# Pooled attention and a snake layer on one core: other places for loads, a store, filler products and a normalisation

## The chip, the cores and the metric

The kernel runs on one core of one Trainium2 chip. The time is the device time of one execution in microseconds (us). Of the kernel before there are ten executions; their median is 920.99 us, the lowest 916.61 and the highest 925.30.

The engines of the core are TensorE (PE in the profile; PEld is its loading of weights), VectorE (DVE), ScalarE (ACT), GpSimd (POOL) and SyncE (SP), whose only work here is to issue DMAs. Each has its own stream of instructions and works through it in order. They wait for each other by semaphores.

## What is computed

Two layers follow each other, in float32 throughout. In the first, k and v are averaged over groups of 8 positions, so that 576 positions become 72, and all 576 queries of each of 8 batches and 8 heads attend to them. In the second, the 4608 rows of 512 numbers go through a layer of 2048 hidden units.

```python
batch, n_heads, seq, head_dim = (8, 8, 576, 64)
k_p = k.reshape(B, H, Sp, pool, D).mean(axis=3)          # pool = 8, Sp = 72
v_p = v.reshape(B, H, Sp, pool, D).mean(axis=3)
scores = scale * np.matmul(q, k_p.transpose(0, 1, 3, 2))
scores = scores - np.max(scores, axis=-1, keepdims=True)
attn = np.exp(scores)
attn = attn / (np.sum(attn, axis=-1, keepdims=True) + 1e-09)
x = np.matmul(attn, v_p).transpose(0, 2, 1, 3).reshape(B * S, H * D)
h = x @ w_in                                             # 4608 x 512 by 512 x 2048
s = np.sin(alpha * h)
out = (h + s * s / (alpha + 1e-09)) @ w_out              # 2048 x 512
```

## The kernel before

**The second layer sets the frame.** The rows of x are taken in nine tiles u of 512 rows. Both of its matrix products use a scheme with 7 products of half-size blocks in place of 8. `hidden` (from L742) walks through 28 slots for each u: four groups J of hidden units, seven products k in each, in the order 1, 5, 6, 2, 7, 3, 4. A slot's product is 4 matmuls of 128x256, each of two passes (L767). Its operands are blocks of w_in or sums of them (`combine_w_in`, L638, which writes the tiles s1, s2, a21 and s4 of a group), and blocks of x or differences of them (`sums_of_x`, L740).

What ScalarE and VectorE do with a product's result is put off by one slot: `left0` to `left6` are the seven pieces (copies of partial sums, adds L746, sine, square), and piece k is written out at the start of slot k+1. `left1` finishes the group before (`finish`, L834), and `left2` stores it into a buffer in DRAM (`store_g`, L841), from which a last phase (`outputs`, L1087) reads it.

**The first layer is spread over these slots.** `carry(u)` says what is put ahead of which slot's product; for each u it prepares the attention of batch b = u+1. In their order: the score products (`two_scores`, L289, two bursts of 32 and 48 short matmuls), row maxima and differences (L312, L313), exponentials (L338), sums and the product with their reciprocals (`norm`, L344 to L346, the last on GpSimd), transposes of the weights in blocks of 32 (`turn`, L472 to L482), 16 DMAs that put the turned blocks in place (`move`, L492), and the products with v (`all_values`, L565 and L578), which write the next tile of x. `k_t` (L251) transposes the pooled k of the batch after next for its scores.

k and v are loaded in halves of a batch (L108; L131 and L139) and pooled by three adds on GpSimd (`pool_rows`, L120). k's and v's first parts share a pool of two buffers, "kvin". The queries are loaded (L80, L96), turned by VectorE and 16 more DMAs (`turn_q`, L212, L219). All these DMAs are issued by SP in the order in which they are written, and SP waits in place when one of them must wait. It is not tied to the slots otherwise: a DMA whose data are there is issued as soon as those ahead of it are.

**The first batch has its own code.** `first_batch` loads k, q and v of batch 0 by pairs of heads, and TensorE pools and transposes them (`k_head` L355, `k_last` L361, `q_head` L372, `sum_v_rest` L182, `sum_v_rows` L192). For each of four pairs follow the products (`products_head`, L393), `soft_shift` (maximum L399 and difference L401), `soft_exp` (L407) and `norm_head` (sum L413, reciprocal L414, two multiplications L419). `a_head` transposes the weights (L447, copied by L449; the last eight keys L455, L456), and `values` (L535, L537) multiplies them with v; `to_x` (L506) copies the result to x. The first half of x is made in `first_batch`, the second in slot 2 of u = 0. Six products of the identity with itself (`warm`, L868), whose results are not used, stand ahead of it in two groups of three, around the transpose of alpha (L600).

The whole order is written by hand; no scheduler changes it.

Of the kernel before, what the change touches and what calls it, by code (L numbers as in the profile page):

```python
# [13 lines left out]
F32 = mybir.dt.float32  # L14
# [26 lines left out]
class Kernel:  # L41
# [79 lines left out]

    def load_v(self, b, i):

        nc, D, H = self.nc, self.D, self.H
        if b not in self.vp:
            self.vp[b] = self.ap.tile([P, H // 2, D], F32, name="vm", bufs=2), self.ap.tile([P, H // 2, D], F32, name="vz", bufs=2)
        vm, vz = self.vp[b]
        if i == 0:
            t = self.kvp.tile([P, 2048], F32, name="kvin")[:].rearrange("p (h x) -> p h x", h=4)
            for s in range(2):  # L130
                nc.sync.dma_start(out=t[64 * s:64 * s + 64],  # L131
                                  in_=self.v[b, 4 * s:4 * s + 4, 0:4 * P, :].rearrange("h (p t) d -> p h (t d)", t=POOL))
            self.pool_rows(t, vm[:])
            return
        x = self.kvp.tile([P, POOL * D], F32, name="vr", bufs=1)[:]
        for s in range(2):
            for c in range(2):
                r = 64 * s + 32 * c
                nc.sync.dma_start(out=x[r:r + 32], in_=self.v[b, 4 * s:4 * s + 4, 4 * P:, :].rearrange("h (k t) d -> h k (t d)", t=POOL))  # L139
        self.pool_rows(x, x[:, 0:D])  # L140
        nc.gpsimd.tensor_tensor(out=vz[:], in0=x[:, 0:D].unsqueeze(1).to_broadcast([P, H // 2, D]),
                                in1=self.mask[:].unsqueeze(2).to_broadcast([P, H // 2, D]), op=OP.mult)

# [87 lines left out]
    def attention(self, b):  # L231
# [208 lines left out]

        def a_head(g, banks, between=None):

            aM, aR = a0_views()
            for e in range(2):
                ps = self.psum([P, 4, P], banks[e])
                for t in range(4):
                    nc.tensor.transpose(ps[:, t, :], self.a0[:, t, 2 * g + e].rearrange("p s k -> p (s k)"), self.ident[:])  # L447
                cp = nc.vector.tensor_copy if g and e else nc.scalar.copy
                cp(out=aM[:, 2 * g + e, 0:4 * P], in_=ps.rearrange("k t n -> k (t n)"))  # L449
            if between:  # L450
                between()
            ps = self.psum([P, 4, P], banks[2])
            w = 64 * g + 64
            for t in range(4):
                nc.tensor.transpose(ps[:w, t, :], self.z0[:, t].rearrange("p hp x k -> p (hp x k)")[:, 0:w], self.ident[:])  # L455
            nc.scalar.copy(out=aR[w - 64:w, 0:4 * P], in_=ps[w - 64:w].rearrange("k t n -> k (t n)"))  # L456
# [36 lines left out]

        def to_x(ps, hp, t0, m, s0=0):

            while s0 < m:
                u, x0 = divmod(b * S + t0 + s0, 2 * TH)
                w = min(m - s0, 2 * TH - x0)
                if u not in self.xT:
                    self.xT[u] = self.home(u % 3, [P, self.K1, 2 * TH])  # L500
                x = self.xT[u][:, hp, x0:x0 + w]
                if t0:
                    y = ps[..., s0:s0 + w]
                else:
                    x, y = x.rearrange("p (j t) -> p j t", t=4), ps[:, s0 // 4:(s0 + w) // 4, :]
                nc.scalar.mul(out=x, in_=y, mul=1.0 / POOL)  # L506
                s0 += w
# [20 lines left out]

        def values(hps, banks, n=1):

            ps = [self.psum([P, 4 * P], i) for i in banks]
            parts = [value_parts(hp, False) for hp in hps]
            for o, (main, _) in zip(ps, parts):
                for e, (w, x) in enumerate(main):
                    nc.tensor.matmul(o[64 * e:64 * e + 64], w, x, start=True, stop=False, skip_group_check=True)  # L535
            for o, (_, (w, x)) in zip(ps, parts):
                nc.tensor.matmul(o, w.rearrange("p e d -> p (e d)"), x, start=False, stop=True, skip_group_check=True)  # L537
            for i in range(n):
                for hp, o in zip(hps, ps):
                    to_x(o.rearrange("p (t j) -> p j t", t=4), hp, 0, 512 // n * (i + 1), 512 // n * i)  # L540

# [189 lines left out]

    def sums_of_x(self, u, n):

        nc = self.nc
        if u not in self.bt:
            self.bt[u] = self.home(3, [P, 4, 2, TH])
        xT, bt = self.xT[u], self.bt[u]
        B = lambda i, j: xT[:, 2 * i:2 * i + 2, j * TH:(j + 1) * TH]
        o, x, y = ((0, B(0, 1), B(0, 0)), (1, B(1, 1), bt[:, 0]), (2, B(1, 1), B(0, 1)), (3, B(1, 0), bt[:, 1]))[n]
        nc.vector.tensor_tensor(out=bt[:, o], in0=x, in1=y, op=OP.subtract)  # L740

    def hidden(self, u, extra):  # L742
# [5 lines left out]
        for slot in range(7 * self.NJ):  # L748
# [51 lines left out]

            def left2(G=G, Q=before):
                if Q:
                    self.store_g(Q)
                G.b7 = bank()
                nc.scalar.copy(out=G.b7[:], in_=G.b6[:])
                G.p5 = self.tp.tile([P, JW, TH], F32, name="p5")
                nc.scalar.copy(out=G.p5[:], in_=G.b5[:])
# [7 lines left out]

            def left5(G=G):
                add(G.g[:, 0, :, 1], G.b6[:], G.p5[:])
# [34 lines left out]
    def first_batch(self):  # L852
# [12 lines left out]
        add_k = [self.load_k_heads(0, nc.sync, nc.vector)]  # L865
        one = self.sm.tile([P, 1], F32, name="one")
        nc.scalar.activation(out=one[:], in_=self.ident[:, 0:1], func=AF.Sqrt)
        warm = lambda n, i: [nc.tensor.matmul(self.psum([P, P], i), self.ident[:], self.ident[:], start=True, stop=True) for _ in range(n)]  # L868
        warm(3, 3)
        self.turn_alpha()  # L870
# [12 lines left out]
        for hp in range(1, 4):  # L883
            add_k.append(self.load_k_heads(hp, nc.sync, nc.vector if hp < 2 else nc.gpsimd))
            self.load_q_heads(0, 2 * hp, 2 * hp + 2)
        add_rest()
        self.load_v_rows(0, h[0][:], self.tp.tile([P, self.DM], F32, name="p5")[:])
# [3 lines left out]
        A.new_a()  # L891
        warm(3, 3)
        A.k_head(0)
        A.q_head(0)
        A.k_last()
        for f in add_k[1:]:
            f()
        A.products_head(0)
        A.k_head(1)
        A.q_head(1)  # L900
        A.soft_shift(0)
        refine()
        A.q_head(2)
        A.products_head(1)
        A.soft_exp(0)
        A.soft_shift(1)
        A.norm_head(0, nc.gpsimd)
        A.k_head(2)
        A.q_head(3)
        A.soft_exp(1)  # L910
        A.products_head(2)
        A.norm_head(1, nc.vector)
        A.k_head(3)
        A.soft_shift(2)
        A.products_head(3)
        A.soft_exp(2)
        self.sum_v_rest(0, 0)
        A.soft_shift(3)
        A.norm_head(2, nc.gpsimd)
        self.sum_v_rows(0, 0, 2)  # L920
        A.a_head(0, (1, 7, 0), lambda: A.soft_exp(3))
        self.sum_v_rows(0, 1, 2)
        A.norm_head(3, nc.gpsimd)
        self.load_q_rest(0, self.q_rest)
# [3 lines left out]
        self.load_w_in_part(1)  # L928
        A.values((0, 1), (4, 1), 2)
        self.combine_w_in(0, (0, 1))  # L930
        self.combine_w_in(0, (2, 3), nc.gpsimd)
        self.sums_of_x(0, 0)

    def carry(self, u):
# [5 lines left out]
        if u == 0:  # L940
            A0, A = self.att[:2]
            at(2, A0.rest_q)
            at(2, A0.a_head, 1, (5, 6, 7))
            at(2, self.half_k)
            at(2, A0.values, (2, 3), (2, 1))
            at(2, self.sums_of_x, 0, 1)
            at(2, A0.score, 4)
# [8 lines left out]
            at(4, A.k_t)  # L956
            at(7, self.load_v, 1, 0)
            at(7, self.load_v, 1, 1)
            for i in range(2):
# [5 lines left out]
            for i in range(4):  # L965
                at((9, 9, 15, 15)[i], A.exp, i)
                at((10, 10, 16, 16)[i], A.norm, i)
                at((13, 13, 17, 19)[i], A.turn, i)
            at(8, self.combine_w_in, 2, (0, 1, 2, 3), self.nc.gpsimd)
            at(10, self.combine_w_in, 3, (0, 1, 2, 3), self.nc.gpsimd)  # L970
            at(17, A0.norm_rest)
            at(23, A0.a_rest)
            at(24, lambda: A0.values_rest((5, 6, 7, (self.turn + 1) % 5)))
            for r in (32, 96):
                at(3, self.nc.gpsimd.memset, self.aM[r:r + 32, :, 704:736], 0.0)
            at(19, A.move, 0)
            at(19, A.move, 1)
            at(26, A.all_values)
# [9 lines left out]
        if 0 < u < last:  # L988
# [8 lines left out]
            at(14, A.move, 0)  # L997
            at(14, A.move, 1)
            for i in range(2):
                at((0, 1)[i], self.load_v, b, i)  # L1000
                if b < last:
                    at(12, self.load_k, b + 1, i)
            at(25, A.all_values)
# [327 lines left out]
```

## Time and profile before

| | us |
|---|---|
| median of ten executions | 920.99 |
| the profiled execution, its own time | 919.92 |
| its span, from the first to the last instruction | 918.1 |
| first product of `hidden` (L767) starts | 21.95 |
| value products of batch 1 (L565) start | 84.55 |
| value products of batch 2 start | 140.54 |
| last product of `hidden`, first phase, ends (start of the last phase, L1087 alone) | 537.1 |

The profile is of one execution. A line of a timeline or of the chain of waits begins with the start and the duration in us, counted from the start of the span; then come engine, line, operation, what is written and read, the number of instructions that were put together, and in brackets how long the engine had been idle and what ended that. "SPq" is SP issuing DMAs. A line of windows gives a stretch, its length, the busy time of PE, PEld, DVE, ACT and POOL with the number of instructions, then the granted share of the TensorE clock, the busy share of the 16 DMA engines and what they moved in GB/s. A matmul's end is modelled, so starts say more than durations there.

The DMA engines are busiest at the start: 0.98 of the first 45 us, in which 255 GB/s are moved; between 104 and 400 us their share is 0.57 to 0.69.

### The profile page before, as it was taken

The page shows a single profiled execution, that of the slowest core. Times are in us where ns is not written, and L with a number is a line of the kernel's source. Part 1 is how long each engine was busy: PE and PEld are TensorE (multiplying, and loading weights), DVE is VectorE, ACT ScalarE, POOL GpSimd, SP SyncE. Part 2 cuts the span into 40 slices and gives each one's busy share as a digit, 9 for nine tenths or more (in the row PEclk, how much of TensorE's full clock was granted, in tenths as well). Part 3 has the DMA queues.
Part 4 walks back from the last instruction along what each step waited for, and adds up shares of the span by engine and source line. Part 5 has one row for each costly group of instructions (what it writes and reads, how often), then busy time and mean ns, then how long its engine had stood idle before and what let it go on. Part 6 is the DMA issues. An engine that isn't in the chain of part 4 may idle for free.

```text
span 918.1 us, 17704 instructions
## 1 busy us (share of the span) xinstructions
PE 901.4 (98%) x7001; PEld 818.3 (89%) x7001; DVE 667.5 (73%) x1005; ACT 435.4 (47%) x997; POOL 162.7 (18%) x155
## 2 busy tenths in 40 slices
PE   8999999999999999999999999999999999999997
PEld 6786887887878888888888899999999999999997
DVE  7674766746667566673466889978888888979894
ACT  5595685866758667586886631112111112111111
POOL 4694250612507034040000000000000000000000
PEclk9999999999999999999999999999999999999999
DMA  9957666766666656637327237171617263533401
GB/s 254 246 190 190 186 175 179 217 177 187 196 171 203 177 155 167 187 93 263 136 92 247 92 107 223 37 224 26 223 37 191 68 170 89 161 98 120 139 14 39
DMA packets 134730, 141.12 MB, mean 154 GB/s; under 512 B 49832, under 2 KB 103224, under 8 KB 134648
## 3 DMA queue, kind: packets, MB, share of 16 engines
q1 hardware_dynamic: 133304, 138.54, 51.9%
q10 hardware_dynamic: 1344, 1.45, 0.6%
q8 instruction: 55, 0.90, 0.4%
q14 instruction: 27, 0.22, 0.1%
HBM read 75.37 MB, written 47.19 MB: 133 GB/s over the span
## 4 chain that ended last, share of the span: by engine, by line
PE 89%; DMA 4%; SPq 3%; POOL 2%; issue 1%; DVE 0%; ACT 0%; POOLq 0%; ACTq 0%
PE PS L767 43%; PE PS L1087 41%; PE PS L565 2%; PE PS L289 2%; DMA a<-in_moe_w_in_dram 2%; DMA kvin<-in_k_dram 1%; DMA kvin<-in_v_dram 1%; SPq L632 1%; POOL as L638 1%; PE PS L578 1%; SPq L492 0%; POOL kvin L120 0%; POOL ex L346 0%; SPq L96 0%; DMA aM<-tr 0%
## 5 line engine op out<-in xcount | busy, mean ns | idle before, releaser
L767 PE MATMUL PS<-home,a 128*128 128x256 f32 x1152 | 264.4, 381 | 0.9 <-ACT home L506 0.5
L767 PEld LDWEIGHTS PS<-home,a 128*128 128x128 f32 x1152 | 216.5, 190 | 37.4 <-issue 5.0
L767 PE MATMUL PS<-home,as 128*128 128x256 f32 x864 | 200.3, 381 | 2.9 <-issue 1.6
L767 PEld LDWEIGHTS PS<-home,as 128*128 128x128 f32 x864 | 162.7, 190 | 26.5 <-issue 2.6
L1087 PE MATMUL PS<-s,wb 128*128 128x144 f32 x896 | 119.3, 286 | 0.4 <-ACT PS L1200 0.4
L1087 PEld LDWEIGHTS PS<-s,wb 128*128 128x128 f32 x896 | 113.7, 190 | 0.7 <-ACT PS L1200 0.6
L780 ACT ACTIVATE s<-s,c 128x256 f32<-128x256 f32 (+1 forms) x216 | 110.0, 572 | 0.0
L746 DVE TENSOR_TENSOR h<-PS,p 128x512 f32<-128x512 f32 x72 | 49.2, 684 | 78.5 <-PE PS L767 45.5
L120 POOL TENSOR_TENSOR kvin<-kvin 96x768 f32<-96x768 f32 (+3 forms) x40 | 66.4, 1661 | 186.7 <-DMA kvin<-in_v_dram 180.2
L773 ACT ACTIVATE s<-h,al 128x256 f32<-128x256 f32 x144 | 65.1, 502 | 55.7 <-DVE h L746 55.0
L1200 ACT COPY PS<-PS 128x144 f32<-128x144 f32 x56 | 14.7, 263 | 146.0 <-PE PS L1087 144.6
L773 ACT ACTIVATE s<-PS,al 128x256 f32<-128x256 f32 x144 | 60.0, 467 | 35.3 <-PE PS L767 17.6
L1087 PE MATMUL PS<-r,wb 128*128 128x144 f32 x512 | 73.2, 286 | 0.0
L1087 PE MATMUL PS<-s,a 128*128 128x144 f32 x512 | 73.2, 286 | 0.0
L834 DVE TENSOR_TENSOR h<-PS,s 128x512 f32<-128x512 f32 x36 | 24.7, 685 | 63.4 <-ACT s L780 63.4
L1087 PEld LDWEIGHTS PS<-r,wb 128*128 128x128 f32 x512 | 67.1, 190 | 0.1
L1087 PEld LDWEIGHTS PS<-s,a 128*128 128x128 f32 x512 | 67.1, 190 | 0.0
L1219 ACT COPY PS<-PS 128x144 f32<-128x144 f32 x56 | 14.7, 263 | 88.2 <-PE PS L1087 88.2
L1087 PE MATMUL PS<-s,we 128*128 128x144 f32 x384 | 54.9, 286 | 0.0
L1087 PE MATMUL PS<-x,wb 128*128 128x144 f32 x384 | 54.9, 286 | 0.0
L1087 PEld LDWEIGHTS PS<-s,we 128*128 128x128 f32 x384 | 50.4, 190 | 0.1
L1087 PEld LDWEIGHTS PS<-x,wb 128*128 128x128 f32 x384 | 50.3, 190 | 0.0
(187 smaller groups left out, 1192.4 us busy)
## 6 DMA issues: line engine op xcount, KB each, us to landing
g_bridge<-h SPq DMA_DIRECT2D x72, 512.0 KB
r<-g_bridge SPq DMA_DIRECT2D x31, 1152.0 KB
out_dram<-o SPq DMA_DIRECT2D x128, 72.0 KB
kvin<-in_k_dram SPq DMA_DIRECT2D x14, 576.0 KB
q<-in_q_dram SPq DMA_DIRECT2D x7, 1024.0 KB
kvin<-in_v_dram SPq DMA_DIRECT2D x14, 512.0 KB
aM<-tr SPq DMA_DIRECT2D x56, 92.0 KB
aM<-tr SPq DMA_DIRECT2D x56, 88.0 KB
```

The costliest lines, as they stand in the source:

```text
L120: self.nc.gpsimd.tensor_tensor(out=t[..., 0:w] if w > D else out, in0=t[..., 0:w], in1=t[..., w:2 * w], op=OP.add)
L289: nc.tensor.matmul(ps[e][r0 + r:r0 + r + q.shape[-1], h, :], q[s], kb[s, hp, :], start=True, stop=True)
L565: nc.tensor.matmul(o[r:r + 64], w, x, start=start and i < 2, stop=False, skip_group_check=True)
L578: nc.tensor.matmul(ps[hp], w.rearrange("p e d -> p (e d)"), x, start=False, stop=True, skip_group_check=True)
L746: add = lambda o, x, y: nc.vector.tensor_tensor(out=o, in0=x, in1=y, op=OP.add)
L767: nc.tensor.matmul(ps[:, jj, :], self.A[p][:, kk, f * P:(f + 1) * P], x[:, kk, :], start=(start and jj == 0 and kk == 0), stop=(kk == 1), ...
L773: nc.scalar.activation(out=G.s[:, i, jj, j, :], in_=src[:, jj], func=AF.Sin, scale=self.al[:, f:f + 1])
L780: nc.scalar.activation(out=x, in_=x, func=AF.Square, scale=self.c[:, f:f + 1])
L834: add = lambda o, x, y: self.nc.vector.tensor_tensor(out=o, in0=x, in1=y, op=OP.add)
L1087: nc.tensor.matmul(out, W[:, J // 2, J % 2, :], A[:, J, :], start=(start and J == 0), stop=(J == self.NJ - 1), skip_group_check=True)
L1200: nc.scalar.copy(out=x1[:, 0, :], in_=x0[:, 1, :])
L1219: nc.scalar.copy(out=x1[:, 1, :], in_=x1[:, 0, :])
```

## The change

There are five kinds of edits.

- In `first_batch`, `warm` gives way to `fill`, which multiplies a tile of ones by itself into a corner of PSUM. 5 such products stand ahead of the transpose of alpha, 4 behind it, and 2 ahead of each pair's products; one more, of 128x512, stands behind the first values. k_last's sums are made later, `q_head` of each pair stands directly ahead of its products, the last normalisation goes from GpSimd to VectorE, and `a_head` is written ahead of the last two exponentials.
- In u = 0, what was put ahead of slot 2 (the rest of q, `a_head` of the second half, the second half of k) goes ahead of slot 1; the second `values` gives one of its results to VectorE, and `sums_of_x` is made in two halves.
- In u = 0, `norm_rest` goes from slot 17 to 13, the combining of group 3 from slot 10 to 14 and 17, and the last `turn` and both `move` from slot 19 to 18.
- For u = 1 to 6, v is loaded ahead of slot 6 instead of 0 and 1, and pooled ahead of slot 12, behind the four `norm`. The store of the last group of u-1 is written in `left5` instead of `left2`.
- For u = 1 to 5, the second half of k is loaded ahead of slot 17 instead of 12, so behind the moves.

On SP the order for u = 1 to 6 was: moves of q, v, store, q. It is: moves of q, store, v, q.

```diff
-    def load_v(self, b, i):
+    def load_v(self, b):
...
+        def pool():
+            self.pool_rows(t, vm[:])
+            self.pool_rows(x, x[:, 0:D])
+            nc.gpsimd.tensor_tensor(out=vz[:], in0=x[:, 0:D].unsqueeze(1).to_broadcast([P, H // 2, D]),
+                                    in1=self.mask[:].unsqueeze(2).to_broadcast([P, H // 2, D]), op=OP.mult)
+        self.pool_v = pool
...
-        def to_x(ps, hp, t0, m, s0=0):
+        def to_x(ps, hp, t0, m, s0=0, eng=nc.scalar):
...
-                nc.scalar.mul(out=x, in_=y, mul=1.0 / POOL)
+                if eng is nc.scalar:
+                    nc.scalar.mul(out=x, in_=y, mul=1.0 / POOL)
+                else:
+                    nc.vector.tensor_scalar(out=x, in0=y, scalar1=1.0 / POOL, scalar2=None, op0=OP.mult)
...
-    def sums_of_x(self, u, n):
+    def sums_of_x(self, u, n, kk=slice(0, 2)):
...
-        nc.vector.tensor_tensor(out=bt[:, o], in0=x, in1=y, op=OP.subtract)
+        nc.vector.tensor_tensor(out=bt[:, o, kk], in0=x[:, kk], in1=y[:, kk], op=OP.subtract)
...
+            late = G.J == 0 and 0 < u < self.B - 1
+
-            def left2(G=G, Q=before):
-                if Q:
+            def left2(G=G, Q=before, late=late):
+                if Q and not late:
                     self.store_g(Q)
...
-            def left5(G=G):
+            def left5(G=G, Q=before, late=late):
+                if late:
+                    self.store_g(Q)
...
+        full = self.tp.tile([P, P], F32, name="full")
+        nc.vector.memset(full[:], 1.0)
...
-        warm(3, 3)
+
+        def fill(n):
+
+            for _ in range(n):
+                nc.tensor.matmul(self.PS[:, 0, 3 * P:4 * P], full[:], full[:], start=True, stop=True)
+        fill(5)
         self.turn_alpha()
...
-        add_rest()
...
-        warm(3, 3)
+        fill(4)
         A.k_head(0)
+        add_rest()
         A.q_head(0)
...
+        fill(2)
         A.products_head(0)
...
-        A.q_head(2)
         A.products_head(1)
-        A.soft_exp(0)
-        A.soft_shift(1)
-        A.norm_head(0, nc.gpsimd)
         A.k_head(2)
+        A.q_head(2)
+        A.soft_shift(1)
+        A.soft_exp(1)
+        A.norm_head(0, nc.gpsimd)
+        fill(2)
+        A.products_head(2)
...
-        A.a_head(0, (1, 7, 0), lambda: A.soft_exp(3))
+        self.sum_v_rows(0, 0, 2)
+        A.a_head(0, (1, 7, 0))
+        A.soft_exp(2)
+        A.soft_shift(3)
+        A.soft_exp(3)
         self.sum_v_rows(0, 1, 2)
-        A.norm_head(3, nc.gpsimd)
+        A.norm_head(2, nc.gpsimd)
+        A.norm_head(3, nc.vector)
...
-        A.values((0, 1), (4, 1), 2)
-        self.combine_w_in(0, (0, 1))
+        A.values((0, 1), (5, 6), (nc.scalar, nc.scalar), 2)
+        nc.tensor.matmul(self.psum([P, 4 * P], 4), full[:], far[0][:, 0:4 * P], start=True, stop=True)
+        self.combine_w_in(0, (0,))
+        self.sums_of_x(0, 0)
+        self.combine_w_in(0, (1,))
...
-            at(2, A0.rest_q)
-            at(2, A0.a_head, 1, (5, 6, 7))
-            at(2, self.half_k)
-            at(2, A0.values, (2, 3), (2, 1))
-            at(2, self.sums_of_x, 0, 1)
+            at(1, A0.rest_q)
+            at(1, A0.a_head, 1, (5, 7, 2))
+            at(1, self.half_k)
+            at(2, A0.values, (2, 3), (2, 1), (self.nc.vector, self.nc.scalar))
+            for kk in range(2):
+                at(2, self.sums_of_x, 0, 1, slice(kk, kk + 1))
...
-                at((13, 13, 17, 19)[i], A.turn, i)
+                at((13, 13, 17, 18)[i], A.turn, i)
...
-            at(10, self.combine_w_in, 3, (0, 1, 2, 3), self.nc.gpsimd)
-            at(17, A0.norm_rest)
+            at(13, A0.norm_rest)
+            at(14, self.combine_w_in, 3, (0, 1), self.nc.gpsimd)
+            at(17, self.combine_w_in, 3, (2, 3), self.nc.gpsimd)
...
-            at(19, A.move, 0)
-            at(19, A.move, 1)
+            at(18, A.move, 0)
+            at(18, A.move, 1)
...
+            at(6, self.load_v, b)
+            at(12, lambda: self.pool_v())
             for i in range(2):
-                at((0, 1)[i], self.load_v, b, i)
                 if b < last:
-                    at(12, self.load_k, b + 1, i)
+                    at((12, 17)[i], self.load_k, b + 1, i)
```

## The prediction

> **What bounds the kernel now.** I read the page first, then the chain of waits, then one-microsecond windows around each gap that the chain shows, then the timeline there. Line numbers are those of the kernel before.
>
> ```profile
> span 918.1 us, 17704 instructions
> PE 901.4 (98%) x7001; PEld 818.3 (89%) x7001; DVE 667.5 (73%) x1005; ACT 435.4 (47%) x997; POOL 162.7 (18%) x155
> PE 89%; DMA 4%; SPq 3%; POOL 2%; issue 1%; DVE 0%; ACT 0%; POOLq 0%; ACTq 0%
> q8 instruction: 55, 0.90, 0.4%
> ```
>
> TensorE is busy for 98% of the span, so this change, which takes no product away, can win only time in which TensorE stands still or runs slowly. The chain in order of time shows where that is:
>
> ```profile
> 81.62 2.12 DMA aM<-tr
> 83.74 0.81 issue
> 84.55 3.69 PE PS L565 x40
> 88.25 0.47 issue
> 88.72 1.19 PE PS L578 x8
> ...
> 140.54 2.51 PE PS L565 x42
> 143.05 1.07 PE PS L578 x8
> ...
> 218.14 1.62 issue
> ...
> 330.22 1.21 issue
> ```
>
> The value products of batch 1 (L565) wait for the moves until 84.55; TensorE had been idle since 82.45. They then take 3.69 us where those of the next batch take 2.51. The windows say why: the granted clock (the number after the five engines) falls just after the gap.
>
> ```profile
> 82.40:84.50 2.10, 0.06 (x1) 0.00 (x0) 0.07 (x1) 0.04 (x1) 0.46 (x1) 1.00 0.70 200
> 86.00:88.00 2.00, 2.00 (x28) 1.73 (x20) 2.00 (x4) 0.01 (x1) 0.00 (x0) 0.50 0.45 160
> ```
>
> The two "issue" gaps are of another kind. The timeline of batch 4:
>
> ```profile
> 209.80 1.32 SPq L131 DMA_DIRECT2D kvin<-in_v_dram  x2
> 210.50 1.33 PE L289 MATMUL PS<-kblk,q 64*64 64x72 f32 x64
> 214.01 0.92 SPq L841 DMA_DIRECT2D g_bridge<-h  x2
> 215.41 1.67 PE L289 MATMUL PS<-kblk,q 64*64 64x72 f32 x96
> 219.77 1.02 PE L767 MATMUL PS<-home,as 128*128 128x256 f32 x4 [1.62 <-issue]
> ```
>
> v is asked for 0.7 us before the score products, which pass through 160 matmuls and as many weight loads; soon after them TensorE stands for 1.62 us with nothing to wait for but its own instructions. The same picture gives the 1.21 us at 330.22. The head:
>
> ```profile
> 1.69 1.65 PE L868 MATMUL PS<-ident 128*128 128x128 f32 x6 [1.69 <-POOL ident masks.py:199]
> 32.30 0.92 PE L767 MATMUL PS<-home,as 128*128 128x256 f32 x3 [1.25 <-DVE home L740]
> ```
>
> **What the Trainium skill says.** "TensorE: Matmul & The Clock Gate", Part 1: the clock is halved unless the array was busy in a free-running window of about 3.4 us, and the phase differs between executions. The trace agrees: half clock from about 85.4 to 88.9, and 128-column products of the head start 0.21 us apart until about 6.9 us, 0.11 us afterwards. "Runtime: NRT & Kernel Launch", Instruction fetch mechanics: instructions come in 16 KiB blocks of 256, fetched by an engine's own DMA queue while it works on the block before. The page's q8 row is that: 55 packets, 0.90 MB, 16 KB each. "DMA: Bandwidth & Descriptors", Queues, rings and completion order, says a DMA engine takes turns between its queues by whole packets, so such a fetch can be held up by a loaded queue; no view prices that by itself.
>
> **The change, part by part.**
>
> *Fillers and the new order of the head.* The first fillers read a tile of ones that VectorE writes after its four constants (the last, L1262, runs 2.38 to 2.65); about 0.2 us for the write, as the 128-column copies of VectorE take 0.17 to 0.28. So TensorE starts near 2.87, not 1.69. Five fillers are ten passes at 0.213 us plus 0.16 for the first: 5.15, where the alpha transpose (L600, before at 3.27) follows. VectorE's chain from it to the first k sums took 4.99-3.27=1.72 us, so these come at 6.88; the second four fillers (8 passes, 1.9 us) end at 7.2. The k products start at about 7.15 instead of 5.05, but the clock is full by then: they and the q transposes take 0.9 us instead of 1.77. k_last now waits for sums that VectorE makes only after the copy of the first pair (two of 0.29, one product 0.3, one copy 0.23). First pair of products: 9.3 instead of 7.70, +1.6. From there the chain is VectorE's as before (reduce 0.75, subtract 0.76, refine 1.5, the sums), and it stays 1.6 behind. Two fillers between pairs cost 0.45 us each and lie in waits for ScalarE's copies (before: 0.49, 0.24, 0.82). Putting the turned weights (two copies 1.07, one 0.57) ahead of the two exponentials (0.70 each) saves the values one exponential, but a_head now waits for the second norm on VectorE (17.85) and the second row sum stands ahead of the values. I get values at 20.75 (before 19.33), their last products at 21.8 to 22.9, and from there the same 1.6 us to the first product of hidden: 23.4 instead of 21.95. **+1.45 us.** Bounds +0.7 to +2.5, by the phase of the clock window.
>
> *Slots 1 and 2 of u=0.* The transposes of the second half (0.39+1.03+0.5 us) now come ahead of slot 1's product (1.9), which covers their three copies; before, the value products waited for these (0.5 us of L535's 1.57). The last evictions run on two engines at once and the difference is made in halves of 0.4: from the last value product to the third hidden product 2.35 us instead of 3.03. VectorE's long reduce (L113, 2.83) ends near 30.3, before it is needed at 31.1. From first product to third: 1.9+1.9+1.9+1.0+2.35 = about 8.9 us instead of 10.35: **-1.45**. So the third product stands at 32.3 again; bounds -0.7 to +1.5 for head and slots together. Loads are not moved by this: the DMA share is 0.98 over the first 45 us, so v lands at 45.5 as before.
>
> *POOL and VectorE in slots 13 to 20 of u=0.* norm_rest moves ahead and half of combine 3 behind the norms. The norms stay at about 66.4, because they wait for VectorE's sums (66.35), and end at 69.3. The last transposes (1.48 us) no longer stand behind an add (L746, 0.69): they start at 69.3 instead of 70.07. So the moves start 0.77 earlier. In exchange this add is 1.2 us late, and slot 20's product waits for it (70.21 becomes 71.45). The moves issue in 11.36 us, to 82.05; values start at 83.8 instead of 84.55 (**-0.75**). TensorE now arrives there at 83.7, since 1.25 of its wait lies at slot 20. Two short gaps instead of one of 2.1 us should leave the clock at full: from L565 to the second hidden product after it took 7.73 us here (84.55 to 92.28) and 5.75 for batch 2 (140.54 to 146.29): **-2.0**. A 1.25 us gap at 31 us did not halve the clock, which is why I take it so.
>
> *v and the late store, u=1 to 6.* SP runs ahead of the slots, so what counts is its order: moves of q, then the store, then v. The store waits for VectorE's finish (L834, over at 211.6 in batch 4), so nothing is asked for from 209.8 to 211.6, and v from 212.6. The block of instructions that failed to come in time was called for within the first score burst (its packet, in the trace's DMA records, starts at 216.88, in v's tail); the twelve added products shift the blocks by 48 instructions, still into that burst. It then meets an empty queue: **-1.62 and -1.21**. v lands about 3 us later; its pooling, now behind the norms, runs from about 123.4 to 130.1 for batch 2 (6.7 us), needed at 140.5. Cover 10 us.
>
> *Half of k behind the moves, u=1 to 5.* It is asked for after the moves and one store (issued 135.93 to 136.97 in u=1), so at 137.05. Store (1.05 MB) and half (0.59 MB) at the 350 GB/s that other windows reach: landed near 141.6. POOL adds 3.49 us (2.90+0.59, as at 123.36): 145.1. k_t stands at 146.0 on TensorE, and everything of slot 26 is queued behind it. Slack 0.9 us; POOL took up to 4.34 beside VectorE, so 0 to 0.5 us per batch: I take **+0.5** for five.
>
> Sum, against the profiled execution (919.92 us, span 918.1): +1.45-1.45-0.75-2.0-2.83+0.5 = -5.1, or 914.8. The median of the runs is 1.07 higher; the clock's phase and the fetch gaps, which vary, may be part of it, so I carry half over: 915.5.
>
> **Rivals.**
> 1. *The gains halve.* The fetch waits only move to other blocks (store, v and q now lie together behind the second burst), or the later start of the head isn't won back. For it: the head's waits are short, and the queue carries as many bytes. Against: 320 instructions lie in the bursts, behind them a block lasts more than 20 us. Time: 914.8+2.8+0.5 = 918.2.
> 2. *Slower: k_t waits for POOL.* One mechanism: the second half of k is summed too late. For it: in u=0 a pair of halves issued at 66.39 landed only at 74.93. If a half lands 7 us after its issue (144.1), POOL is done at 147.7, 1.7 us after TensorE reaches k_t: five times, +8.5. Time 924. It makes the kernel slower from about 1.6 us per batch on, and eats all gain at 1.
> 3. *Better*: full clock reaches the head earlier and VectorE's chain is shorter than I have it (+0.5 instead of +1.45), no wait for k: 912.5.
>
> **How the numbers follow.** Likeliest case 0.52 (913 to 918), rival 1 0.24, rival 2 0.13, rival 3 0.11. What a measurement of this kernel can tell is 0.3%, 2.8 us: faster is under 918.2. Faster: 0.50 of the likeliest, 0.11, and a third of rival 1 (0.08), less 0.03 for what I have not seen: 0.66. Same: most of rival 1 and a bit of 2: 0.20. Slower: 0.14. The range takes rival 3 and most of rival 1 and stops short of rival 2: 911.5 to 921.
>
> **What would show it.** Right: no "issue" gap of over 1 us on TensorE behind the second burst; granted clock 1.00 from 84 to 90; first hidden product near 23.4, third near 32.3; slot 20 waiting for L746. Wrong: TensorE idle before L251 in u=1 to 5, ended by POOL or VectorE; first hidden product past 25; new "issue" gaps.

## The result, and the profile after

The changed kernel is slower by half a per cent. Its median is 926.43 us (923.16 to 928.97, 14 runs) beside 921.93 us of the kernel before on the same chip: ratio 1.0051, 95% interval 1.0034 to 1.0067. Ratios here and below leave out executions that lie more than 1.5% above the fastest of their kernel, which bears on `e3_no_fill` alone (five of its 22). Its profiled execution took 924.81 us, with a span of 923.0 (before: 919.92 and 918.1). Line numbers of this part are those of the changed kernel unless said otherwise; up to `to_x` they lie one below those of before, from `finish` on four above, and most between are the same.

Three lines of the page: span, busy time of each engine, and the shares in the chain of waits.

```profile
span 923.0 us, 17756 instructions
...
PE 905.9 (98%) x7025; PEld 820.9 (89%) x7025; DVE 668.8 (72%) x1010; ACT 435.7 (47%) x996; POOL 159.6 (17%) x153
...
PE 86%; DVE 4%; SPq 3%; DMA 2%; POOL 1%; issue 1%; ACT 1%; DVEq 0%; POOLq 0%; ACTq 0%
```

VectorE had 0% of the chain and now has 4%. The chain in order of time, from 200 to 345 us, has one "issue" entry among its longest pieces, where the two of 1.62 and 1.21 us had stood:

```profile
236.57 0.35 issue
```

So the two waits that the prediction put down to instruction fetches are gone, and the loss is elsewhere. Landmarks of both executions by their timelines, start in us (the changed kernel makes the third product's operand in two parts; the first two of the product's eight matmul passes need only the first part, and the line "its third pass" shows the next):

| | before | after | difference |
|---|---|---|---|
| products of the first pair | 7.70 | 10.48 | +2.78 |
| products of the fourth pair | 13.97 | 18.58 | +4.61 |
| values of the first two pairs | 19.33 | 23.35 | +4.02 |
| hidden product 1 | 21.95 | 26.39 | +4.44 |
| hidden product 3 | 32.30 | 37.90 | +5.60 |
| its third pass | 32.83 | 39.31 | +6.48 |
| hidden product of slot 4 | 36.98 | 45.17 | +8.19 |
| all_values of batch 1 | 84.55 | 91.94 | +7.39 |
| of batch 2 (its first matmul) | 140.47 | 146.34 | +5.87 |
| of batches 3, 4, 5, 6, 7 | | | +6.60, +5.08, +5.59, +4.34, +4.82 |
| end of the span | 918.1 | 923.0 | +4.9 |

Eight us are lost by slot 4, and three are won back later. Each column is one execution; how far such landmarks move by themselves is said under "Why the prediction was wrong". TensorE's timeline in the head (start, duration, and in brackets the idle time before and what ended it):

```profile
2.84 2.50 PE L878 MATMUL PS<-full 128*128 128x128 f32 x10 [2.84 <-DVE full L872]
...
9.62 0.43 PE L360 MATMUL PS<-twos,home 128*128 128x64 f32 x2 [0.73 <-DVE home L152]
...
10.48 0.73 PE L392 MATMUL PS<-h,q 64*64 64x72 f32 x32
...
26.39 1.89 PE L767 MATMUL PS<-home,a 128*128 128x256 f32 x8
...
30.38 1.99 PE L767 MATMUL PS<-home,as 128*128 128x256 f32 x8 [0.25 <-DVE home L740]
...
37.90 0.70 PE L767 MATMUL PS<-home,as 128*128 128x256 f32 x2 [1.91 <-DVE home L740]
39.31 2.93 PE L767 MATMUL PS<-home,as 128*128 128x256 f32 x6 [0.71 <-DVE home L740]
```

The third product waits 1.91 us for the first half of its operand and 0.71 for the second; and after these two gaps the clock halves, as the first number behind the five engines shows:

```profile
39.30:42.50 3.20, 3.19 (x8) 2.57 (x9) 2.79 (x6) 0.17 (x1) 1.08 (x1) 0.50 0.80 182
...
88.00:90.00 2.00, 2.00 (x15) 1.74 (x10) 0.00 (x0) 0.99 (x6) 1.36 (x2) 1.00 0.59 142
```

What VectorE does meanwhile is in its timeline, beside GpSimd's:

```profile
26.57 3.21 POOL L120 TENSOR_TENSOR kvin<-kvin 96x768 f32<-96x768 f32 x2
26.61 2.31 DVE L638 TENSOR_TENSOR as<-a,a 128x512 f32<-128x512 f32 x1
28.84 1.48 DVE L740 TENSOR_TENSOR home<-home 128x512 f32<-128x512 f32 x1
...
30.25 2.29 DVE L638 TENSOR_TENSOR as<-as,a 128x512 f32<-128x512 f32 x1
...
30.74 1.26 POOL L638 TENSOR_TENSOR a<-a,a 128x512 f32<-128x512 f32 x1
32.47 0.68 DVE L448 COPY aM<-PS 128x512 f32<-128x512 f32 x1
...
33.07 2.82 DVE L113 TENSOR_REDUCE kp<-kvin 96x192 f32<-96x1536 f32 x1
...
36.30 1.26 POOL L638 TENSOR_TENSOR as<-as,a 128x512 f32<-128x512 f32 x1
36.52 2.74 DVE L740 TENSOR_TENSOR home<-home,home 128x256 f32<-128x256 f32 x2
37.52 1.45 POOL L638 TENSOR_TENSOR a<-a,a 128x512 f32<-128x512 f32 x1
```

The same four pieces of work in the kernel before (its timeline, its line numbers):

```profile
20.83 0.85 DVE L638 TENSOR_TENSOR as<-a,a 128x512 f32<-128x512 f32 x1
21.71 0.69 DVE L638 TENSOR_TENSOR as<-as,a 128x512 f32<-128x512 f32 x1
22.75 1.10 DVE L740 TENSOR_TENSOR home<-home 128x512 f32<-128x512 f32 x1 [0.35 <-ACT home L506]
...
31.55 0.69 DVE L740 TENSOR_TENSOR home<-home,home 128x512 f32<-128x512 f32 x1 [0.60 <-ACT home L506]
```

Together 3.33 us before and 2.31 + 1.48 + 2.29 + 2.74 = 8.82 after. In this stretch only operations with two operands in SBUF grew. The copy from PSUM (L448, 0.68; 0.69 before) and the long reduce (L113, 2.82; 2.83 before) did not. Taken apart, the two adds of L120 end at 28.37 and 29.78, and VectorE's first two operations at 28.92 and 30.32, each 0.55 later: they look like operations that cannot end before GpSimd's instruction has. The Trainium skill says so of this pair ("SBUF — State Buffer", Who interferes with whom): VectorE with two SBUF inputs and GpSimd reading SBUF take turns at a shared port by whole instructions, and a reduce stays out of it. The prediction did not look there. The experiments ask whether this is the loss.

### The profile page after: what moved, and what is told of

It reads as the page before. It is cut to its first block, busy times and chain, and to the rows that moved or that the text cites. A ratio compares the mean times of both kernels' runs of the same rounds, so it can differ in the third digit from the quotient of the medians.

```text
span 923.0 us, 17756 instructions
## 1 busy us (share of the span) xinstructions
PE 905.9 (98%) x7025; PEld 820.9 (89%) x7025; DVE 668.8 (72%) x1010; ACT 435.7 (47%) x996; POOL 159.6 (17%) x153
## 3 DMA queue, kind: packets, MB, share of 16 engines
q10 hardware_dynamic: 1344, 1.45, 0.6%
## 4 chain that ended last, share of the span: by engine, by line
PE 86%; DVE 4%; SPq 3%; DMA 2%; POOL 1%; issue 1%; ACT 1%; DVEq 0%; POOLq 0%; ACTq 0%
PE PS L1107 42%; PE PS L767 39%; SPq L489 3%; PE PS L288 2%; DMA kvin<-in_k_dram 2%; PE PS L565 1%; POOL kvin L120 1%; DVE tr L469 1%; PE PS L878 0%; PE PS L578 0%; DVE home L740 0%; DVE sm L343 0%; ACT s L780 0%; DVE h L746 0%; SPq L845 0%
## 5 line engine op out<-in xcount | busy, mean ns | idle before, releaser
L746 DVE TENSOR_TENSOR h<-PS,p 128x512 f32<-128x512 f32 x72 | 49.1, 684 | 80.5 <-PE PS L767 46.5
L120 POOL TENSOR_TENSOR kvin<-kvin 96x768 f32<-96x768 f32 (+3 forms) x40 | 63.1, 1579 | 47.8 <-DMA kvin<-in_k_dram 41.7
L345 POOL TENSOR_TENSOR ex<-ex,sm 128x576 f32<-128x576 f32 (+1 forms) x28 | 35.0, 1271 | 182.6 <-ACT PS L807 163.8
```

The costliest lines, as they stand in the source:

```text
L120: self.nc.gpsimd.tensor_tensor(out=t[..., 0:w] if w > D else out, in0=t[..., 0:w], in1=t[..., w:2 * w], op=OP.add)
L345: nc.gpsimd.tensor_tensor(out=E(i), in0=E(i), in1=sm.unsqueeze(2).to_broadcast([P, n, Sp]), op=OP.mult)
L746: add = lambda o, x, y: nc.vector.tensor_tensor(out=o, in0=x, in1=y, op=OP.add)
```

## The experiments

All were timed beside the kernel before, those whose names begin with the same letter on the same chip; so ratios, not times, are compared between e, f and g. Each has one profile.

### Which half of the change loses

`e1_head_before` is the changed kernel with `first_batch` and what stands ahead of slots 1 and 2 of u = 0 as before; `e2_late_only` is the kernel before with only the edits of `load_v`, the late store and the half of k for u = 1 to 6.

```diff
 e1: in carry, u == 0 (and first_batch as before)
-            at(1, A0.rest_q)
-            at(1, A0.a_head, 1, (5, 7, 2))
-            at(1, self.half_k)
+            at(2, A0.rest_q)
+            at(2, A0.a_head, 1, (5, 6, 7))
+            at(2, self.half_k)
```

> The first batch's code and what is put ahead of slots 1 and 2 of u=0 are as before; all other edits stay. If the loss lies in the head, the third product of hidden is back near 32.3 us, the value products of batch 1 start at 83.5 to 84.5, the clock stays full there, the waits of L250 remain (1.5 to 2 us in all), the two gaps of 1.2 to 1.6 us do not return, and the time is 917 to 919 (ratio to before 0.994 to 0.997). If the edits of u=1 to 6 cost more than they bring, the ratio stays at 1.000 or above.

> The kernel before with only v and the late store behind the scores and half of k behind the moves, u=1 to 6. If these win the two fetch gaps (2.8 us) and lose 1.6 to 2 us before L251, the ratio is 0.998 to 1.000 and the profile shows no gap of over 1 us behind the second score burst. If they are the cause of the loss, the ratio is over 1.002.

Measured: e1 918.88 us, ratio 0.9979 [0.9965, 0.9993]; e2 918.97 us, 0.9978 [0.9962, 0.9994]. Both are a little faster than before. So the late edits win some 2 us, the head with slots 1 and 2 loses what lies between e1's ratio and the change's, 0.7%, and the edits of slots 13 to 20, which e1 has and e2 has not, add nothing that can be told between the two. In e1's profile hidden products 1 and 3 start at 21.18 and 31.54, and L250 still waits 0.92, 0.27, 0.35 and 0.46 us.

### The last normalisation

`e4_norm3_pool` changes one word of the changed kernel.

```diff
-        A.norm_head(3, nc.vector)
+        A.norm_head(3, nc.gpsimd)
```

> The changed kernel with the last normalisation of batch 0 back on GpSimd. If VectorE's queue between 23 and 33 us is what holds the second and third product, it loses 1.06 us there and its first two combinations meet GpSimd's multiplications instead of its pooling of k (0.7 to 1.1 us each as before, not 2.3): the third product comes 2 to 4 us earlier, time 923 to 924. If the turned weights of the second half must wait for GpSimd's second multiplication instead, it comes no earlier.

Measured: 919.88 us, ratio 0.9988 [0.9973, 1.0003], by the ratios 5.8 us under the changed kernel and more than expected. Its timeline:

```profile
23.96 3.44 POOL L418 TENSOR_TENSOR tr<-ex,sm 128x512 f32<-128x512 f32 x4 [6.21 <-DVE sm L413]
24.60 0.94 DVE L638 TENSOR_TENSOR as<-a,a 128x512 f32<-128x512 f32 x1
25.87 1.38 DVE L740 TENSOR_TENSOR home<-home 128x512 f32<-128x512 f32 x1 [0.32 <-ACT home L504]
27.17 0.78 DVE L638 TENSOR_TENSOR as<-as,a 128x512 f32<-128x512 f32 x1
...
33.79 0.76 DVE L740 TENSOR_TENSOR home<-home,home 128x256 f32<-128x256 f32 x2
```

The first two weight combinations and the first difference start 2 to 3 us earlier and take 0.94, 0.78 and 1.38 us beside GpSimd's short multiplications (0.74 to 1.04 each); the halves of the last difference take 0.76 together. Hidden products 1, 2 and 3 start at 25.49, 29.06 and 34.26, slot 4's at 38.94, and the clock stays full. From the first product to the third it is 8.77 us, where the changed kernel has 11.51. The normalisation itself is 1.06 us of VectorE, so four fifths of the 5.8 us are not its own duration.

That leaves two readings: VectorE meets GpSimd's longer work because it comes later, or the queue is late for a reason of its own. Two kernels keep the normalisation on VectorE and change GpSimd. `f2_pool_quiet` only writes GpSimd's pooling of k and two combinations later in the program; `g1_pool_held` makes them wait for the operand of product 3.

```diff
-        self.load_k(1, 0)
+        self.pool_k = self.load_k(1, 0, 'pool')
...
-        self.combine_w_in(0, (2, 3), nc.gpsimd)
...
+            at(2, lambda: self.nc.gpsimd.tensor_copy(out=self.sm.tile([P, 1], F32, name="held")[:], in_=self.bt[0][:, 1, 1, 0:1]))
+            at(2, self.combine_w_in, 0, (2,), self.nc.gpsimd)
+            at(2, lambda: self.pool_k())
+            at(2, self.combine_w_in, 0, (3,), self.nc.gpsimd)
```

> The changed kernel, last normalisation on VectorE, but GpSimd's pooling of the first half of k and its two combinations of group 0 stand only behind the values of slot 2. If VectorE is slowed by GpSimd working beside it, its two combinations take 0.7 to 0.9 us each instead of 2.3 and its difference 0.7 instead of 1.5, the second and third product come 3 to 4 us earlier (third near 34.5), and the time falls to 920 to 922. If it is only the 1.06 us more in VectorE's queue and its order, they stay within 1 us of 37.9 and the time stays at 925 to 927.

Measured: 924.76 us, ratio 1.0041 [1.0028, 1.0054], and it decides nothing: nothing ahead in GpSimd's queue waits, so the pooling still ran from 25.11 to 29.3 and VectorE's operations still took 2.31, 1.48, 2.30 and 2.75 us. To be later in the program is not to be later in time.

> The changed kernel with one thing put off: GpSimd's pooling of the first half of k (3.2 us) and its two combinations of the first group's weights are held by a one-column copy that reads the operand of the third hidden product, so GpSimd does nothing while VectorE makes the operands of products 2 and 3; the last normalisation stays on VectorE. Theory (the two engines keep each other waiting: it is not the normalisation's own 2.8 us that costs 6.5, but that it pushes VectorE's two-input operations under GpSimd's work): L638 takes 0.9 and 0.75 instead of 2.31 and 2.29, the halves of L740 0.8 together instead of 2.74; product 2 at 29 instead of 30.4, product 3 near 34.7 instead of 39.3; some of it is given back since the pooling that k_t needs now ends only near 39.5: all_values 88 to 90 instead of 91.9, time 921 to 924.5, ratio to before 0.999 to 1.003. Rival (the operations are slow or late on VectorE for a reason of their own, the normalisation ahead of them alone): durations as in the changed kernel, product 3 at 38 to 39.5, and the late pooling is a pure loss: 927 to 930.

Measured: 922.98 us, ratio 1.0014 [0.9998, 1.0030]. Its timeline (two lines further down in the numbering):

```profile
25.15 0.68 DVE L640 TENSOR_TENSOR as<-a,a 128x512 f32<-128x512 f32 x1
25.76 0.68 DVE L742 TENSOR_TENSOR home<-home 128x512 f32<-128x512 f32 x1
26.36 0.68 DVE L640 TENSOR_TENSOR as<-as,a 128x512 f32<-128x512 f32 x1
...
33.24 0.76 DVE L742 TENSOR_TENSOR home<-home,home 128x256 f32<-128x256 f32 x2
33.72 1.99 PE L769 MATMUL PS<-home,as 128*128 128x256 f32 x8 [0.59 <-DVE home L742]
...
35.44 4.20 POOL L122 TENSOR_TENSOR kvin<-kvin 96x768 f32<-96x768 f32 x2
...
40.35 0.47 PE L252 MATMUL PS<-ident,kp 96*128 96x96 f32 x3 [2.04 <-POOL kp L122]
```

With GpSimd quiet, and the normalisation still ahead of them on VectorE, the four take 2.80 us instead of 8.82, and product 3 starts 8.78 us behind product 1 instead of 11.51. This shows the mechanism. Most of the win is lost at once, as the held pooling is now what k_t waits for (2.04 us, L252), and the clock is half from 40.9 to 44.3 behind that gap. The profile also shows the other direction: the held L122 adds take 4.20 us where the two of L120 take 2.88 in the kernel before, beside two operations of L742 at 35.62 and 36.22 (0.67 and 0.68 us).

### The fillers and the order of the pairs

`e3_no_fill` is the changed kernel without the fillers between pairs, without the 128x512 product, and with 3 + 3 products of the identity in place of 5 + 4. The 128x512 product is no mere filler: by the program it writes the bank of PSUM in which the first group's third hidden product then accumulates on a copy. `e3` leaves that write out, and its values are not those of the other kernels, so only its time is of use.

```diff
-        fill(5)
+        fill(3)
...
-        fill(2)
...
-        nc.tensor.matmul(self.psum([P, 4 * P], 4), full[:], far[0][:, 0:4 * P], start=True, stop=True)
```

> The changed kernel with the products of before in place of the fillers (three of the identity on each side of the alpha transpose, none between pairs, none behind the values). If the fillers' later start carries the head's loss, the first product of hidden starts near 24 us instead of 26.4 and the third near 36 instead of 38 to 39, and the time falls by 2 to 3 us to 923 to 924. If VectorE's work beside GpSimd's carries it, the first product moves but the third stays within 1 us of 38, and the time falls by less than 1 us.

Measured: 928.04 us, ratio 1.0052 [1.0025, 1.0078]; neither expectation came true. Of its 22 runs 18 lie at 926.6 to 929.9 and four at 915.4 to 919.5, below every run of the changed kernel. The profiled one is of the many, with hidden product 1 at 28.82; its timeline:

```profile
8.18 1.24 PE L392 MATMUL PS<-h,q 64*64 64x72 f32 x32 [0.41 <-DVE h L361]
...
11.99 1.24 PE L392 MATMUL PS<-h,q 64*64 64x72 f32 x32 [0.68 <-ACT q L372]
```

32 score products take 1.24 us where they take 0.73 in the changed kernel: half clock until 24.3 us, where the changed kernel's is full from 8.5. So in this order of the head the fillers bring the full clock early. The four short runs have no profile; that they found the full clock early without fillers is likely but not shown. Why the order needs fillers the changed kernel's chain suggests:

```profile
12.23 0.46 PE PS L371 x4
12.71 0.59 ACT q L372
13.35 0.73 PE PS L392 x32
14.08 0.59 PE PS L354 x4
14.67 0.46 PE PS L371 x4
15.15 0.59 ACT q L372
15.79 0.73 PE PS L392 x32
```

Transposes of q, their copy on ScalarE, products, the next pair's k, and so on: one after the other. Before, the q transposes of some pairs stood a pair ahead, and pair followed pair after 2.44, 1.69 and 2.14 us; now it is 2.87, 2.44 and 2.79.

Two kernels start from e4. `f3_q_ahead` puts the transposes of q one pair ahead; `f4_ident_fill` has 3 + 3 identity products in place of the 5 + 4 of the full tile, and keeps those between pairs.

```diff
 f3
         A.q_head(1)
+        A.q_head(2)
         A.soft_shift(0)
...
         A.k_head(2)
-        A.q_head(2)
+        A.q_head(3)
 f4
-        fill(5)
+        fill(3, self.ident)
```

> The changed kernel with the last norm on GpSimd, and the transposes of q one pair ahead as before the change. If the pairs are slow because transpose, copy and products of a pair now follow each other (3.3, 2.4, 2.8 us from pair to pair against 2.4, 1.7, 2.1), the pairs come 0.5 to 0.8 us closer, the first product of hidden comes 1.2 to 2 us earlier (near 24 against 25.5) and the time falls by as much, to 918. If VectorE's chain sets the pace, nothing moves by more than 0.3 us.

> The changed kernel with the last norm on GpSimd, and in place of the nine fillers of ones around the alpha transpose six of the identity, as before; the fillers between pairs stay. If the late start (2.84 against 1.69) and the three more fillers push the head, the first pair's products come at 8.0 to 8.3 instead of 9.8, the first product of hidden near 24, and the time falls by 1 to 1.5 us. If the clock then gets full later in many runs, the time rises or spreads by 4 us or more.

Measured: f3 920.10 us, 0.9998 [0.9979, 1.0017]; from the first pair to the fourth it is 7.53 us instead of 8.51, and hidden product 1 is at 24.73 instead of 25.49, which the time does not resolve. f4 918.72 us, 0.9974 [0.9962, 0.9986]; the first pair's products at 8.66 instead of 9.77, but with the clock full only from 12.6 us (e4: 7.5) the second follows after 3.92 us instead of 3.28, and hidden product 1 is at 25.02. Both gains are smaller than expected.

### The second half of k

In the changed kernel (timeline of u = 1):

```profile
142.63 0.82 SPq L108 DMA_DIRECT2D kvin<-in_k_dram  x1
...
148.82 2.88 POOL L120 TENSOR_TENSOR kvin<-kvin 96x768 f32<-96x768 f32 x2 [8.30 <-DMA kvin<-in_k_dram]
151.77 0.59 POOL L120 TENSOR_TENSOR kp<-kvin 96x192 f32<-96x192 f32 x1
...
152.42 0.47 PE L250 MATMUL PS<-ident,kp 96*128 96x96 f32 x3 [0.67 <-POOL kp L120]
```

GpSimd starts on the half 6.2 us after its issue, which stands behind a store, and TensorE waits 0.67 us for its sums; in later batches 0.34 and 0.57. `g2_k_early` asks for it directly behind the moves and ahead of that store, all else as changed; `f1_old_head_k_early` does this with `first_batch` as before and slots 1 and 2 as changed.

```diff
             at(14, A.move, 0)
             at(14, A.move, 1)
+            if b < last:
+                at(14, self.load_k, b + 1, 1)
...
-                    at((12, 17)[i], self.load_k, b + 1, i)
```

> The changed kernel with the second half of k asked for directly behind the moves and ahead of the store, all else as changed. Theory (the waits at L250 of 0.67, 0.34 and 0.57 us and what lies around them cost the 1.95 us that the changed kernel loses over five batches): no wait ahead of L250, the head as changed (products 26.4, 30.4, 39.3), time 2 us under the changed kernel: 924.0 to 925.0, ratio to before 1.002 to 1.004. Rival (k's place costs nothing of it and the loss over five batches is another's): 926 to 927, ratio 1.0045 to 1.006.

> First batch as before, slots 1 and 2 of u=0 as changed, and the second half of k asked for directly behind the moves, ahead of the store. If the waits of L250 come only from the half's late landing, they go (under 0.3 us in all against 1.6 to 2 us), the third product of hidden comes near 30.7 us (8.8 us after the first, as with the last norm on GpSimd), and the time is 915 to 917 (ratio 0.994 to 0.997). If the half lands no earlier because the moves still fill the queues, L250 waits as before and the ratio is 0.997 to 0.999.

Measured: g2 922.33 us, ratio 1.0007 [0.9987, 1.0028], with no wait ahead of L250. Its head is as late as the changed kernel's (products 26.93, 30.91, 38.44); from the first value products to the end it takes 828.8 us, the changed kernel 831.1. That is the 2 us expected; the medians differ by 4, with intervals that allow either. f1: 916.00 us (7 runs), ratio 0.9946 [0.9926, 0.9967], hidden products at 22.99 and 31.88, no wait ahead of L250. It beats both kernels. In its timeline the half is asked for at 134.36 and GpSimd starts on it 5.2 us later:

```profile
139.54 3.13 POOL L120 TENSOR_TENSOR kvin<-kvin 96x768 f32<-96x768 f32 x2 [6.66 <-DMA kvin<-in_k_dram]
...
142.75 0.59 POOL L120 TENSOR_TENSOR kp<-kvin 96x192 f32<-96x192 f32 x1
...
144.21 0.41 PE L250 MATMUL PS<-ident,kp 96*128 96x96 f32 x3
```

### The three together

`g3_three_mended` is the changed kernel with the edits of e4, f4 and g2.

> The changed kernel with three edits together: the last normalisation on GpSimd, identity products 3+3 in place of 5+4 of the full tile ahead of the pairs, second half of k directly behind the moves. If the three sizes add (6.5, 1.2 and 2.0 us under the changed kernel): 916.5 to 917.5, ratio to before 0.995 to 0.9965, hidden products near 25.0/28.6/33.8, no wait ahead of L250, clock full throughout. If k's place is hidden once the head is short: 918 to 919, ratio 0.997. The kernel with the old head and k early (916.0) remains the yardstick: this one begins its hidden products 2 us later and can't be under it unless the pairs' start doesn't set the end.

Measured: 916.56 us (16 runs), ratio 0.9948 [0.9930, 0.9966]. That is 9.5 us under the changed kernel by the ratios, and the three sizes add up to 9.7; the fillers' 1.2 alone, e4 against f4, the intervals do not resolve. The new head, mended, is as good as the old one: hidden product 1 at 25.74 and 3 at 34.52, and full clock from 14.2 us to the end.

## Why the prediction was wrong

It said faster by 5.5 us, and the kernel is slower by 4.5. Its sum, term by term, against the two profiles:

- **Slots 1 and 2 of u = 0, forecast -1.45: the step that failed.** It counted "1.9+1.9+1.9+1.0+2.35 = about 8.9 us" from the first hidden product to the third. Measured are 1.82, 2.17, 1.93, 1.90 and 3.69, in all 11.51, and the third product's other passes follow 1.41 us behind its start, where it was 0.53 before. The last two terms are the ones that broke, both on VectorE. The value products wait for a copy (L448) that VectorE begins only at 32.47, behind L638. The long reduce L113, which was to end before it was needed, ends 9.5 us after product 1 and not 6.9; then the difference, priced "in halves of 0.4", takes 1.3 and 1.5. Missing from the step, and from the prediction altogether, is the last normalisation's move to VectorE: 1.06 us, which put the operations of L638 and L740 under GpSimd's pooling and combinations. Without that meeting the count holds: e4 has 8.77 and g1 8.78.
- **Fillers and the new order of the head, forecast +1.45, at most +2.5: measured +4.44 in this profile, +3.0 in two others.** TensorE starts at 2.84, as forecast (2.87). The first pair comes at 10.48, not 9.3: the clock is full from 8.48 and not from 7.15, and TensorE stands 0.73 us for L152, which takes 0.70 beside GpSimd's add L162 (8.59 to 9.41). Both vary from execution to execution. With the same program up to there, e4, f2, f3 and g1 have L152 at 0.29 and the first pair at 9.49 to 9.77, near the forecast; f2 and g1, with the same head, reach hidden product 1 at 24.94, g2 at 26.93. What all of these but f3 share is the next step: "it stays 1.6 behind" failed. The prediction took VectorE's chain for the pace and put fillers and copies into waits, while the chain shows each pair's transposes, copy and products in series. From the first pair to the fourth it is 8.1 us (8.5 in e4) where it was 6.3. Setting q ahead takes 1.0 of that away (f3 against e4); the rest is taken for the order itself, and no run changed the order alone.
- **A half clock that the sum had not.** Behind the 1.91 and 0.71 us waits of product 3 the clock is half from 39.2 to 42.6; the lag grows from 6.5 to 8.2 us by slot 4. f2 and g2, which have the same waits, have it too; e4, f3, f4 and g3, where product 3 waits 0.59, have not. So it belongs to the first failure.
- **Slots 13 to 20, forecast -0.75: right in this profile.** From slot 4 to the first value products the lag falls by 0.8, slot 20's product waits 1.25 us for L746, and the value products wait for no move.
- **Full clock at 84 to 90, forecast -2.0: a size read from one execution.** The clock is 1.00 there, and the lag falls by 1.5. But the profile of before was itself a chance: e2, whose slots 13 to 20 are as before, waits 1.78 us for the moves at this place, and its clock stays full. In the medians neither this term nor the one before shows: e1 has the edits of slots 13 to 20, e2 has not, and the two are equal within 2 us.
- **The two fetch waits, forecast -2.83: right.** The lag falls by 1.5 and 1.25 at these batches, and in e1 and e2 no such gap is left either. That they were fetches stays the prediction's reading; no run tested it apart from the order of the loads.
- **Half of k, forecast +0.5: mis-sized, +1.7** (0.73, 0.51, 0.48). From issue to its first add the half took 6.2 us, where the prediction had it landed after 4.6; without the store ahead it is 5.2 (f1), so the store is 1.0 of that. Rival 2 named this mechanism and put the landing at 7 us and the loss at 8.5; it is real and a fifth of that.

From slot 4: 8.2 - 0.8 - 1.5 - 2.8 + 1.7 = 4.8, the measured end. Rival 1 named a head that is not won back, but with no size of its own, and no rival held this loss. Two of the signs of being wrong came: hidden product 1 past 25 us, and TensorE idle before `k_t`. Rival 3's 912.5 is also about a us lower than its own terms, which give 913.4. The 915.5 that was forecast is near what the change gives once the normalisation, the fillers' size and the place of k are put right (g3, f1); as the -2.0 in it was not to be had in the median, this is partly luck.

## What to carry to other kernels

When an operation goes to another engine, price not only its own duration but where it pushes what stands behind it: look at what the other engines run in those microseconds, and for two-operand operations on VectorE at what GpSimd runs. A later place in the program moves nothing in time on an engine that waits for nothing. Fillers that cure a half clock in one order of work may be curing only that order: count the serial chain (transpose, copy, product) first. A term read from one profile may be worth nothing in the median: look for the same code in another kernel's profile before putting it into a sum.

## What the runs showed of the hardware

- An operation of VectorE with two float32 operands in SBUF, 128x512, takes 0.68 us with GpSimd quiet (g1). Where it stood for GpSimd's adds of k and weights it took 1.3 to 2.3, and beside its shorter multiplications 0.78 to 1.38. The slowed ones end about 0.55 us after an instruction of GpSimd ends (0.28 for those of 128x256). GpSimd waits in the same way: one combination (1.27 us) took 2.70 in the kernel before, from 33.56, beside two of L740.
- Beginning first did not settle who waits. L638, begun at 30.25 in the changed kernel, ended only 0.55 us after the combination that GpSimd began at 30.74; the combination of 33.56 in the kernel before ended 1.1 us after operations of VectorE that began at 33.86 and 34.46.
- The meeting is not tied to the change. In e2, whose code up to slot 4 is that of the kernel before, GpSimd began at 31.24 a combination that in the kernel before waited for its weights until 33.56. The three operations of L740 took 1.50, 1.28 and 1.75 us instead of 0.69, 0.67 and 0.68, and with a half clock behind them slot 4 began at 39.48 instead of 36.98.
- Gaps of TensorE and the clock: 1.21, 1.25 and 1.62 us (kernel before) and 1.78 (e2) left it full; behind 2.04 (g1), 2.06 (e2), 2.10 (kernel before), and 1.91 and 0.71 close together (changed kernel, f2, g2, e3) it was half for 3.4 us, in g2 and e3 for 6.8. No run varied a gap alone, so these traces give no threshold.
- With 5 + 4 fillers of ones ahead of the first pair the clock was full from 6.4 to 8.5 us on (six profiles), with 3 + 3 products of the identity from 5.2 to 14.2 (six profiles) and, with none between pairs in the new order, 24.3 (e3).
